# Top-k attention and channel mix on one core: the last 64 rows of two head pairs in two shared tiles

## The chip, the cores and the metric

One core of one Trainium2 chip runs the whole program. The metric is device time in microseconds (us), the median of several runs. TensorE (PE), VectorE (DVE), ScalarE (ACT), GpSimd (POOL) and the DMA queue of SyncE (SP) each work through their own instructions in order; semaphores tie them together.

## What is computed

For 8 batches and 8 heads, with 576 rows of 64 numbers: scores q·kᵀ/8, of each row of 576 scores only those not under the 32nd largest are kept, softmax over them, times v. The heads side by side give x (576 rows of 512), and x goes through a channel mix:

```
scores = scale * q @ k.T;  kth = 32nd largest of each row
attn = softmax(where(scores >= kth, scores, -1e9));  x = attn @ v
xk = mu_k*x + (1-mu_k)*x_prev;  xr = mu_r*x + (1-mu_r)*x_prev
out = sigmoid(xr @ w_r) * (relu(xk @ w_k)**2 @ w_v)
```

x_prev is x one row earlier. Everything is float32; the products of the mix are made of three products of split operands (`three`, lines 630 to 632).

## The kernel before

**Attention in tiles of 128 rows.** Heads go in pairs, so that two times 64 channels fill 128 partitions; a batch has four pairs (`hp`). 576 rows of two heads are nine tiles: tiles 0 to 7 alternate between the heads (head `j = i % 2`, 128 rows each), tile 8 holds the last 64 rows of both heads, one above the other. `visits()` lists the work: for each batch the four pairs with tiles 0 to 3, then the four pairs with tiles 4 to 8 (`HALVES`). That is 64 visits and 288 tiles.

**Scores (L815 to L848).** For tiles i and i+1 one `score` makes two products of 64 contraction rows and 512 columns, one head on the upper 64 rows of the array and one on the lower (L843), into two banks of PSUM (`psA`, `psB`). One `sliver` makes the scores against the last 64 keys of both heads (L839), with keys laid out block-diagonally. For tile 8 `score8` multiplies a block-diagonal q (128 x 128) with all keys, 512 + 64 columns (L830, L831). ACT copies each tile to SBUF (`keep`, L848).

**Selection.** DVE finds the 24 largest through seven pieces (`cand` L853, `best` L855, `drop` L858), ACT and POOL mark what lies below (`count` L867, `below` L869), DVE takes eight more (L870), picks the threshold (L872), ACT makes the exponentials (L875), DVE masks and sums them (`mask`, L878).

**Weighing.** PE turns each tile's weights (`turn`, L883), ACT copies them (`et`, L885). The last 64 columns of a pair of tiles are turned together (`turnl` L892, `el` L894); tile 8 has a `turnl` and an `el` of its own. `weigh` (L912, L913) makes ten products per pair of tiles, j = 0 on the left 64 columns of the array, j = 1 on the right ones, 128 columns each, and for tile 8 ten products of 64 columns. The row sums are inverted and spread (`inv` L922, `inv2` L923, `spread` L929), turned (`turni`, L933), copied by ACT (`ri`: L938 for four tiles, two instructions L939 for tile 8), and `place` (L946, L948 for tile 8) writes x in SBUF. All these exist once for tiles 0 to 3, once for 4 to 7 and once for tile 8.

**The mix.** The 4608 rows of x go in 18 chunks of 256 through `mixes`: POOL and ACT make the mixed inputs and split them (L1012 to L1026), PE makes `hidden` (w_k), `gate` (w_r) and `value` (w_v), which run in one chain in the order of the chunks, DVE multiplies (L1069), a DMA stores (L1073). A chunk needs all four pairs' x for its rows. The weights are decoded at the start (L1108 to L1122).

**What sets the order.** Every step is an operation of a planner (`Plan`) with a lane, a cost, a latency and a key. The planner plays the program through with these numbers, always takes the startable operation of smallest key, and the kernel issues instructions in that order. Keys are tile numbers plus offsets by name (`OFF`, and `FIRST`, `HEAD`, `TAIL` for parts of the run); all of these are numbers tuned outside the kernel. Buffers are fixed slots: two of `K` (keys), two of `qs` (queries), two of `v`; a slot is loaded anew when its last reader is done.

Of the kernel before, what the change touches and what calls it, by code (L numbers as in the profile page):

```python
# [13 lines left out]
U16 = mybir.dt.uint16  # L14
# [7 lines left out]
TOPK = 32  # L22
# [15 lines left out]
OFF = dict(kt=-121.428, kq=29.029, v=64.905, zero=125.157, score=-21.076, score8=-233.323, keep=-111.033, cand=4.395, best=-14.048, drop=-234.145,  # L38
           under=-104.819, count=-7.004, below=-87.858, eighth=7.346, nine=-95.487, exps=-2.384, mask=-112.099, turn=-43.368, et=10.16,
           turnl=-32.999, el=-45.066, weigh=-13.326, inv=-38.077, inv2=-154.266, turni=-65.888, ri=48.604, place=-110.038, lowest=85.255,  # L40
           ranks=-161.631, mu=81.53, nmu=-66.769, changek=202.813, sharek=59.24, addk=295.566, xhk=27.059, xlk=-59.888, sharer=146.441, addr=89.379,
           xhr=64.885, xlr=-19.387, hidden=57.882, relu=-325.908, sq=75.222, r2=42.675, hl=89.124, gate=342.639, gexp=-237.14, value=80.824,
           gated=-51.641, store=-26.275, w=151.463, wabs=-23.359, wshift=5.075, wsign=-219.789, wexp=45.53, wfine=-25.33, whi=-128.231, wmul=141.404,
           spread=-76.068, sliver=-106.383, low=-94.304, lowt=146.639, lowr=-225.937, lowc=25.086, wrest=-67.307, wm=184.027, wput=35.385)
CANDS, BESTS = 0.129, -8.186
STEP, WAT, WSTEP, GATE, VALUE, PACE = 21.948, 3.155, 8.557, 3.863, 3.573, -2.0
HALVES = range(4), range(4, 9)
# [19 lines left out]
BONUS = {("S", "W"): -33.152, ("T", "W"): 18.092, ("R", "W"): -33.936, ("T", "S"): 28.628, ("R", "S"): 41.738, ("W", "S"): -27.081, ("S", "R"): 66.373, ("T", "R"): 53.755, ("W", "R"): 68.359, ("R", "R"): 36.687, ("S", "S"): 46.812, ("R", "T"): 21.687, ("W", "W"): -9.529, ("Z", "S"): -113.211, ("W", "Z"): 44.387, ("S", "T"): -26.18, ("Z", "W"): -40.234, ("Z", "R"): 49.709, ("T", "Z"): 90.229, ("S", "Z"): 15.286, ("R", "Z"): 31.114, ("Z", "Z"): -23.831, ("Z", "T"): -8.059, ("W", "T"): 32.559, ("T", "T"): -8.034}  # L67
# [3 lines left out]
NEAR = dict(PE=142.316, ACT=94.901, DVE=1.447, POOL=234.747, SP=6.125)  # L71
LAST, PEAT = "last", 112
LWAT, LWSTEP = 26.429, -3.165
VWAT, VWSTEP = 1.354, 3.543
AT = [-6.03, -8.616, 62.223, 51.725, 69.632, 81.783, 97.48, 87.342, 134.245, 89.408, 140.491, 139.103, 174.089, 182.425, 241.323, 261.83, 194.143, 348.355]
START = 24
FIRST = dict(kt=5.431, kq=3.152, v=-49.962, zero=-7.051, score=-72.928, score8=-89.904, keep=-50.114, cand=30.564, best=-19.859, drop=129.007,
             under=-50.906, count=-109.448, below=29.13, eighth=12.534, nine=10.971, exps=12.953, mask=59.199, turn=-221.857, et=-50.959,
             turnl=-64.196, el=18.176, weigh=-236.035, inv=-23.695, inv2=12.596, turni=-211.084, ri=84.374, place=-108.496, ranks=22.855, mu=-68.04,
             nmu=-170.249, changek=-72.361, sharek=21.572, addk=-131.096, xhk=-23.566, xlk=38.625, sharer=-60.941, addr=151.697, xhr=148.99,  # L80
             xlr=101.845, hidden=50.53, relu=-47.517, sq=23.585, r2=124.261, hl=36.104, gate=-117.566, gexp=-151.448, value=-38.023, gated=138.744,
             store=164.456, w=-17.631, wabs=-242.464, wshift=-71.332, wsign=-114.016, wexp=-28.894, wfine=-150.111, whi=39.513, wmul=-64.181,
             spread=-19.73, sliver=27.977, wrest=45.495, wm=-182.753, wput=-79.997, low=85.741, lowr=-24.363, lowest=116.236, lowc=87.799,
             lowt=-13.95)
HEAD = dict(sharek=-47.371, zero=154.778, lowt=-23.559, score8=-11.785, store=209.645, el=-79.186, gate=-26.338, turni=91.426, sq=26.461, hl=113.15,
            relu=-47.049, wmul=-27.583, low=-6.219, xhk=61.499, inv=110.857, v=-12.116, gated=-131.363, xlk=16.829, turn=42.663, r2=4.269,
            xlr=16.635, addr=-200.707, ri=-66.902, below=-14.314, best=-24.605, wabs=-59.334, lowr=180.774, sliver=-116.326, nmu=14.466, kq=141.279,
            changek=39.743, count=-13.892, hidden=6.777, addk=-98.359, xhr=95.257, lowc=60.575, eighth=-56.451, w=172.797, kt=1.172, wshift=-10.774,
            wexp=15.565, ranks=119.206, spread=32.638, mask=-44.708, whi=179.551, drop=-62.419, gexp=65.164, keep=-94.404, inv2=-20.263, mu=-116.499,
            weigh=-64.727, turnl=48.3, score=-5.275, under=-90.964, nine=-79.706, place=-5.27, sharer=50.724, et=33.131, wfine=30.879,  # L90
            wsign=-118.488, exps=-49.391, lowest=-68.808, value=60.46, cand=6.626, wrest=5.672, wm=2.948, wput=-29.083)
TAIL = dict(addr=75.077, wshift=-71.426, wexp=88.368, sq=220.928, lowt=-151.351, sliver=-126.01, whi=-14.333, xlk=100.276, xhk=54.542, store=-72.657,
            nine=53.016, best=55.339, lowr=9.427, hl=81.731, turni=-109.29, xhr=45.326, relu=-18.048, kt=30.108, drop=85.184, gate=-36.159,
            score8=-63.376, eighth=-43.894, under=-43.046, inv2=-36.699, v=29.142, w=-96.933, wmul=0.662, wfine=26.729, lowest=-64.048, gexp=123.791,
            score=-32.419, sharek=-17.199, wabs=-168.587, exps=2.264, nmu=-196.418, below=26.843, changek=-82.372, lowc=17.854, inv=270.105,
            low=-26.01, gated=77.754, turnl=33.065, place=59.611, ri=124.319, r2=-54.949, weigh=-98.505, spread=-120.091, kq=-22.273, cand=60.211,
            value=5.334, hidden=-50.412, zero=35.483, ranks=-27.964, mu=85.532, count=39.835, mask=101.415, wsign=37.272, xlr=118.137, keep=-40.713,
            addk=3.005, el=-27.772, sharer=-104.183, turn=-6.619, et=-42.42, wrest=30.561, wm=-111.8, wput=-71.442)
# [4 lines left out]
MORE = dict(xh=2, xl=2, et=5, top=3, el=3, eb=3, sg=3, K=2)  # L103
# [84 lines left out]
class Plan:  # L188
# [236 lines left out]
def topk_attention_channel_mix(ctx: ExitStack, tc: tile.TileContext, q, k, v, mu_kr, w_k, w_v, w_r, out):  # L425
# [355 lines left out]
    def attend(plan, visits, X, pair_sums):  # L781
# [6 lines left out]
        seen = None  # L788

        for p, (b, hp, part) in enumerate(visits):  # L790
# [10 lines left out]
            plan.op(ACT if p == 0 else SP, "kq", at0, 500, 2600, lambda P=P, b=b, hp=hp, lo=lo, hi=hi, issue=issue: issue.dma_start(P.qs.t[:, :hi - lo], q[b, hp, :, lo:hi]), writes=[P.qs])  # L801
            P.v = buf("v")
            plan.op(SP, "v", at0, 500, 3800, lambda P=P, b=b, hp=hp: nc.sync.dma_start(P.v.t, v[b, hp]), writes=[P.v])
# [8 lines left out]
            for i in part:  # L812
                n = at0 + i - P.first
                T = Env()
                T.i, T.P = i, P  # L815
                j, u = i % 2, i // 2 % 2
                if i % 4 == 0 or i == P.first:
                    U = Env()
                    U.i = i
                    U.rs, U.weigh = buf("rs"), []  # L820
                    U.w = 1 if i == 8 else min(part[-1], i | 3) + 1 - i
# [3 lines left out]
                if i == 8:  # L825
                    ps, sl = [buf("psA")], buf("sl")

                    def score8(P=P, ps=ps, sl=sl):
                        qd = P.qs.t[:, MAIN - P.first * 64:WIDE - P.first * 64]
                        return [nc.tensor.matmul(ps[0].t, lhsT=qd, rhs=P.K.t[:, :MAIN], start=True, stop=True),  # L830
                                nc.tensor.matmul(sl.t[:, MAIN:S], lhsT=qd, rhs=P.K.t[:, MAIN:S], start=True, stop=True)]  # L831
# [15 lines left out]
                def keep(T=T, x=ps[j] if i < 8 else ps[0], sl=sl, o=960 if j else 0):  # L847
                    return nc.scalar.activation(T.sc.t, sl.t[:, o:o + S], AF.Copy)  # L848
# [436 lines left out]
```

## Time and profile before

| | |
|---|---|
| median of 3 runs | 1171.61 us (1169.31 to 1172.63) |
| the profiled execution, its own time | 1169.51 us |
| its span, first to last instruction | 1167.7 us |
| PE busy | 1096.4 us (94%) |
| DVE busy | 1068.1 us (91%) |
| ACT busy | 1015.9 us (87%) |
| POOL busy | 934.2 us (80%) |
| DMA engines, mean over the span | 78 GB/s, 91.0 MB |

Busy time is the union of the instructions' recorded intervals, and neighbouring instructions overlap by their fixed latencies, so a share near 100% says that an engine always has something under way, not that it can do no more. An average over the span mixes three stages: a start with the decoding of weights, a long middle with attention and mix together, and an end with the mix alone. So the busy times by stage are read first, then single instructions.

### The profile page before, as it was taken

What the parts mean: (1) busy time and instruction counts of PE and PEld (TensorE: products, weight loads), DVE (VectorE), ACT (ScalarE), POOL (GpSimd) and SP (SyncE); (2) the same over time, 40 slices, a digit from 0 to 9 for tenths busy, and PEclk for the clock granted to TensorE, in tenths of its full rate; (3) what the DMA queues carried; (4) which work ended last, traced back from release to release, by engine and by line L of the source; (5) the groups of instructions that cost most, each with busy time, mean ns of one, the idle gap of its engine ahead of it and who ended that gap; (6) DMA issues with size and microseconds to landing.
All of it is one profiled execution on the core that took longest, in us unless ns stands there. A gap on an engine that the chain in (4) does not pass through costs nothing. (4 is left out here: it accounts for less than half of the span.)

```text
span 1167.7 us, 27723 instructions
## 1 busy us (share of the span) xinstructions
PE 1096.4 (94%) x8593; PEld 860.0 (74%) x8593; DVE 1068.1 (91%) x5773; ACT 1015.9 (87%) x2193; POOL 934.2 (80%) x1185
## 2 busy tenths in 40 slices
PE   3566898999999999999999999999999999999998
PEld 1344676877787777878787878787878787878897
DVE  6999999999999999999999999999999999998600
ACT  5888998989898999989899899999998999898641
POOL 4777997868787888888699888888788869787773
PEclk9877999999999999999999999999999999999999
DMA  8644232222122122221221221221221222120000
GB/s 293 227 146 155 86 99 85 67 65 65 58 75 74 58 62 79 67 72 45 86 78 57 60 71 55 75 76 42 87 76 56 60 72 70 60 75 26 19 19 22
DMA packets 38893, 91.00 MB, mean 78 GB/s; under 512 B 4432, under 2 KB 12624, under 8 KB 38736
## 3 DMA queue, kind: packets, MB, share of 16 engines
q1 hardware_dynamic: 38448, 88.75, 24.0%
q8 instruction: 70, 1.15, 0.4%
q14 instruction: 87, 0.71, 0.2%
q10 hardware_dynamic: 288, 0.39, 0.1%
HBM read 79.69 MB, written 9.44 MB: 76 GB/s over the span
## 5 line engine op out<-in xcount | busy, mean ns | idle before, releaser
L869 POOL TENSOR_TENSOR sg<-sc,sg 128x576 f32<-128x576 f32 x288 | 411.1, 1429 | 87.7 <-ACT sg L867 85.7
L853 DVE MAX8 cand<-sc 128x8 f32<-128x82 f32 (+1 forms) x2016 | 375.2, 230 | 6.3 <-ACT sc L848 5.1
L867 ACT ACTIVATE sg<-sc,seen 128x576 f32<-128x576 f32 x288 | 225.1, 782 | 17.6 <-POOL seen L864 15.8
L875 ACT ACTIVATE se<-sc,seen 128x576 f32<-128x576 f32 x288 | 216.5, 752 | 19.4 <-DVE E L878 18.5
L878 DVE SCALAR_TENSOR_TENSOR E<-sc,seen,se 128x576 f32<-128x576 f32 x288 | 230.7, 801 | 0.3
L848 ACT ACTIVATE sc<-ps 128x576 f32<-128x576 f32 x288 | 185.5, 653 | 41.8 <-DVE E L878 21.7
L883 PE MATMUL rot<-ident,E 128*128 128x128 f32 x1152 | 183.1, 285 | 40.5 <-DVE E L878 21.7
L870 DVE MAX8 top<-sg 128x8 f32<-128x576 f32 x288 | 214.6, 745 | 7.0 <-POOL sg L869 6.7
L883 PEld LDWEIGHTS rot<-ident,E 128*128 128x128 f32 x1152 | 132.9, 144 | 105.4 <-DVE E L878 20.7
L855 DVE MAX8 top<-cand 128x8 f32<-128x56 f32 x864 | 176.1, 205 | 2.4
L885 ACT ACTIVATE et<-rot 128x512 f32<-128x512 f32 x288 | 171.1, 601 | 7.3 <-PE rot L883 6.8
L630 PE MATMUL rot<-xh,wk 128*128 128x256 f32 x576 | 169.6, 294 | 0.0
L912 PE MATMUL ps<-et,v 128*64 128x128 f32 (+1 forms) x2560 | 161.5, 269 | 1.8 <-ACT el L894 1.3
L631 PE MATMUL rot<-xl,wk 128*128 128x256 f32 x576 | 160.9, 279 | 0.3 <-POOL xl L1026 0.3
L632 PE MATMUL rot<-xh,wk 128*128 128x256 f32 x576 | 160.8, 279 | 0.0
L843 PE MATMUL ps<-K,qs 64*128 64x512 f32 x512 | 154.9, 684 | 0.2
L912 PEld LDWEIGHTS ps<-et,v 128*64 128x64 f32 x2560 | 132.8, 139 | 25.0 <-issue 8.5
L630 PE MATMUL rot<-wv,hh 128*128 128x512 f32 x288 | 121.3, 421 | 0.0
L858 DVE MATCH_REPLACE8 cand<-top,cand 128x56 f32<-128x56 f32 x576 | 115.2, 200 | 0.4 <-issue 0.4
L630 PEld LDWEIGHTS rot<-xh,wk 128*128 128x128 f32 x576 | 109.6, 190 | 6.4 <-issue 4.5
L632 PE MATMUL rot<-wv,hl 128*128 128x512 f32 x288 | 113.4, 394 | 0.0
L631 PE MATMUL rot<-wv,hh 128*128 128x512 f32 x288 | 112.6, 391 | 0.0
(87 smaller groups left out, 2303.4 us busy)
## 6 DMA issues: line engine op xcount, KB each, us to landing
v<-in_v SPq DMA_DIRECT2D x64, 384.0 KB, 3.1
K<-in_k SPq DMA_DIRECT2D x64, 352.0 KB, 3.0
out<-eb SPq DMA_DIRECT2D x35, 256.0 KB, 2.0
qs<-in_q SPq DMA_DIRECT2D x32, 192.0 KB, 3.2
stage<-in_moe_w_k SPq DMA_DIRECT2D x8, 512.0 KB, 4.9
xT<-in_moe_w_v SPq DMA_DIRECT2D x8, 512.0 KB, 4.6
stage<-in_moe_w_k SPq DMA_DIRECT2D x8, 511.5 KB, 4.7
xT<-in_moe_w_v SPq DMA_DIRECT2D x8, 511.5 KB, 3.6
```

Of the source, the lines that this page charges most:

```text
L630: return [nc.tensor.matmul(ps, lhsT=sh, rhs=mh, start=first, stop=False), nc.tensor.matmul(ps, lhsT=sh, rhs=ml, start=False, stop=False), ...
L631: nc.tensor.matmul(ps, lhsT=sh, rhs=ml, start=False, stop=False),
L632: nc.tensor.matmul(ps, lhsT=sl, rhs=mh, start=False, stop=last)]
L848: return nc.scalar.activation(T.sc.t, sl.t[:, o:o + S], AF.Copy)
L853: lambda T=T, c=c: nc.vector.max(T.cand.t[:, 8 * c:8 * c + 8], T.sc.t[:, CUTS[c]:CUTS[c + 1]]), reads=[T.sc], writes=[(T.cand, c)])
L867: lambda T=T, sn=sn: nc.scalar.activation(T.side.t, T.sc.t, AF.Sign, bias=sn(T, 1), scale=-BELOW, accum_out=T.top.t[:, TOPK:TOPK + 1]),
L869: plan.op(POOL, "below", n, 1375, 1430, lambda T=T: nc.gpsimd.tensor_mul(T.side.t, T.sc.t, T.side.t), reads=[T.sc], writes=[T.side])
L870: plan.op(DVE, "eighth", n, 660, 754, lambda T=T: nc.vector.max(T.top.t[:, 24:32], T.side.t), reads=[T.side], writes=[(T.top, 3)])
L875: plan.op(ACT, "exps", n, 667, 754, lambda T=T, pe=pe, sn=sn: nc.scalar.activation(pe.t, T.sc.t, AF.Exp, bias=sn(T, 0), scale=SCALE), read ...
L878: lambda T=T, U=U, pe=pe, sn=sn: nc.vector.scalar_tensor_tensor(T.e(), T.sc.t, sn(T, 2), pe.t, op0=OP.is_ge, op1=OP.mult, accum_out=U.rs.t ...
L883: return [nc.tensor.transpose(pt.t[:, c * 128:(c + 1) * 128], E.t[:, o + c * 128:o + (c + 1) * 128], ident) for c in range(NKC)]
L912: return [*[nc.tensor.matmul(pa[hs[j]], lhsT=vs[j][:, c, :], rhs=ms[c][j], start=(c == 0), stop=False) for c in range(NKC) for j in range(2)],
```

## The change

The last 64 rows of two neighbouring pairs (`hp` even and odd) are put in two ordinary tiles, 8 and 9, which are worked on in the visit of the odd pair: tile 8 holds head 0 of both pairs, tile 9 head 1. The count of tiles stays 288. `score8` falls away; the score of tiles 8 and 9 is four products of 64 x 64 on the four quarters of the array, their sliver two products on its column halves. `turnl`, `el`, `inv`, `inv2`, `spread`, `turni`, `ri` and `place` exist once where there were two; the two weighings stand in one operation. `v` and `qs` have three slots, and smaller ones, `K` still two. Twelve transposes of the identity run on PE at the start (`warm`). Costs of DMAs in the planner are raised, and all offsets have new values, among them that of `value`, the last product of the mix, 137.781 for 80.824.

```diff
-HALVES = range(4), range(4, 9)
+HALVES = range(4), range(4, 8)
...
-                vs.append((b, hp, part))
+                vs.append((b, hp, range(part[0], 10) if part[0] and hp % 2 else part))
...
-MORE = dict(xh=2, xl=2, et=5, top=3, el=3, eb=3, sg=3, K=2)
+MORE = dict(xh=2, xl=2, et=5, top=3, el=3, eb=3, sg=3)
...
-            lo, hi = P.first * 64, WIDE if full else (part[-1] + 1) * 64
+            lo, hi = P.first * 64, S if full else (part[-1] + 1) * 64
...
-            plan.op(SP, "v", at0, 500, 3800, lambda P=P, b=b, hp=hp: nc.sync.dma_start(P.v.t, v[b, hp]), writes=[P.v])
+            plan.op(SP, "v", at0, 1150, 3400, lambda P=P, b=b, hp=hp: nc.sync.dma_start(P.v.t, v[b, hp, :, :WIDE]), writes=[P.v])
...
-                if i == 8:
-                    ps, sl = [buf("psA")], buf("sl")
...
-                    plan.op(PE_, "score8", n, 1090, 1280, score8, reads=[P.K, P.qs], writes=[*ps, sl], mode="Z")
-                elif j == 0:
+                ends = [before, P] if i >= 8 else [P]
+                if j == 0:
                     ps, sl = [buf("psA"), buf("psB")], buf("sl")
...
+                        if i == 8:
+                            return [nc.tensor.matmul(to[r * 64:(r + 1) * 64], lhsT=X.qs.t[:, MAIN // 2:MAIN // 2 + REST], rhs=X.K.t[:, S:].rearrange("p (h x) -> p h x", h=2), start=True, stop=True)
+                                    for r, X in enumerate(ends)]
...
+                        if i == 8:
+                            return [nc.tensor.matmul(ps[h].t[ws[r]], lhsT=X.qs.t[w, MAIN // 2:MAIN // 2 + REST], rhs=X.K.t[w, :MAIN], start=True, stop=True)
+                                    for r, X in enumerate(ends) for h, w in enumerate(ws)]
...
-                    plan.op(PE_, "score", n, 965, 1155, score, reads=[P.K, P.qs], writes=ps, mode="S")
+                    plan.op(PE_, "score", n, 965, 1155, score, reads=[x for X in ends for x in (X.K, X.qs)], writes=ps, mode="S")
...
+                    if i < 8:
+                        U.weigh.append((weigh, 1140, [t.et for t in es] + [el, P.v], [U.pa[u]]))
+                    else:
+                        U.weigh.append((lambda weigh=weigh, ends=ends: [x for r, X in enumerate(ends) for x in weigh(P=X, r=r)], 1258, [t.et for t in es] + [el] + [X.v for X in ends], U.pa))
...
+                        if U.i == 8:
+                            return nc.vector.tensor_mul(x.t[:, hp - 1:hp + 1, 1 + MAIN:], pair_sums[:, :, :REST], U.ri.t[:, :128].rearrange("p (u q) -> p u q", u=2))
...
-        sizes = dict(v=(2, [128, WIDE + 2 * D]), K=(2, [128, S + 2 * REST]), qs=(2, [128, 384]), ...
+        sizes = dict(v=(3, [128, WIDE]), K=(2, [128, S + 2 * REST]), qs=(3, [128, MAIN // 2 + REST]), ...
...
+            plan.op("PE", "warm", -99, 1300, 1500, lambda: [nc.tensor.transpose(warm.t[:, :128], ident, ident) for _ in range(12)], writes=[warm], mode="T")
```

## Rows read from the trace of the kernel before

**Rows 1.** Busy us (x instructions): window, its length, PE, PEld, DVE, ACT, POOL; PEclk, DMA, GB/s.

```profile
0.00:200.00 200.00, 137.25 (x909) 93.34 (x910) 184.24 (x894) 166.34 (x347) 152.61 (x183) 0.88 0.48 158
...
200.00:1107.00 907.00, 903.66 (x7346) 717.39 (x7347) 880.56 (x4875) 830.45 (x1814) 748.06 (x975) 1.00 0.21 64
...
1080.00:1107.00 27.00, 27.00 (x224) 22.14 (x224) 17.36 (x77) 17.86 (x41) 19.13 (x24) 1.00 0.03 11
1107.00:1163.00 56.00, 55.47 (x346) 49.30 (x342) 2.98 (x6) 19.06 (x35) 33.50 (x29) 1.00 0.06 20
```

**Rows 2.** Timeline where attention ends: start us, length us, engine, line, what, count.

```profile
1100.24 0.42 DVE L946 TENSOR_TENSOR xT<-ps,ri 128x256 f32<-128x256 f32 x1 [1.95 <-PE ps L913]
...
1105.45 2.55 POOL L1026 TENSOR_TENSOR xl<-xm,xh 128x512 fp32r<-128x512 f32 x2
...
1106.99 0.29 PE L913 MATMUL ps<-el,v 128*64 128x64 f32 x4
1107.21 0.39 PE L630 MATMUL rot<-xh,wk 128*128 128x256 f32 x1
```

**Rows 3.** DVE's `cand`: timeline near the start, and its group by line.

```profile
8.36 1.41 DVE L853 MAX8 cand<-sc 128x8 f32<-128x82 f32 x9 [2.25 <-ACT sc L848]
...
L853 DVE MAX8 cand<-sc 128x8 f32<-128x82 f32 x1440 | 291.7, 229 | 6.3 <-ACT sc L848 5.1
```

**Rows 4.** PE timeline of one `score8` and the transpose that follows.

```profile
535.93 1.02 PE L830 MATMUL ps<-K,qs 128*128 128x512 f32 x2
...
536.96 0.39 PE L933 MATMUL rot<-ident,ri 128*128 128x128 f32 x2
```

**Rows 5.** PE timeline of `turn`, `score`, `sliver` and what follows.

```profile
563.06 0.60 PE L883 MATMUL rot<-ident,E 128*128 128x128 f32 x4
563.59 1.13 PE L843 MATMUL ps<-K,qs 64*128 64x512 f32 x4
564.65 0.49 PE L839 MATMUL ps<-K,qs 128*128 128x128 f32 x2
564.89 0.48 PE L630 MATMUL rot<-wv,hh 128*128 128x512 f32 x1
```

**Rows 6.** PE timeline of single transposes and `weigh` of tile 8; one `weigh` of 128 columns.

```profile
560.53 0.27 PE L933 MATMUL rot<-ident,ri 128*128 128x128 f32 x1
560.64 0.27 PE L892 MATMUL ps<-ident,E 128*128 128x128 f32 x1
560.84 0.69 PE L912 MATMUL ps<-et,v 128*64 128x64 f32 x16
561.36 0.29 PE L913 MATMUL ps<-el,v 128*64 128x64 f32 x4
561.57 0.50 PE L630 MATMUL rot<-wv,hh 128*128 128x512 f32 x1
...
568.63 1.09 PE L912 MATMUL ps<-et,v 128*64 128x128 f32 x16
...
569.77 1.04 PE L912 MATMUL ps<-et,v 128*64 128x128 f32 x16
```

**Rows 7.** Groups by line, engine and shape: busy us, mean ns of one, idle before.

```profile
L948 DVE TENSOR_TENSOR xT<-ps,ri 128x64 f32<-128x64 f32 x32 | 6.9, 217 | 2.3 <-ACT ri L939 1.2 <-ACT sc L848 0.5 <-PE ps L913 0.2
```

**Rows 8.** Loads of K: PE and SP timelines, time to landing, a wait on SP's queue.

```profile
499.68 0.59 PE L830 MATMUL ps<-K,qs 128*128 128x512 f32 x1
...
500.47 0.33 SPq L797 DMA_DIRECT2D K<-in_k  x1
...
DMA to landing us min/median/max: 2.8/3.0/5.7
...
SPq L1073 <- DVE eb L1069: 108.3, 10, 28.7
```

**Rows 9.** PE timeline of the first products.

```profile
4.85 0.77 PE L839 MATMUL ps<-K,qs 128*128 128x128 f32 x2 [4.85 <-DMA qs<-in_q]
5.55 2.08 PE L843 MATMUL ps<-K,qs 64*128 64x512 f32 x4
```

More of the change, by code (lines that the diff above doesn't have):

```diff
@@ L37 @@
 BIG = 3.0e38
[L38 to L46, printed above, removed]
-HALVES = range(4), range(4, 9)
+OFF = dict(kt=-121.077, kq=24.149, v=20.84, zero=149.844, score=-39.01, keep=-107.344, cand=5.903, best=-12.044, drop=-198.58, under=-101.486,
+           count=-24.438, below=-113.606, eighth=8.556, nine=-64.432, exps=-9.366, mask=-113.332, turn=-39.888, et=8.524, turnl=-26.569, el=-78.147,
+           weigh=-20.184, inv=-21.087, inv2=-158.168, turni=-57.394, ri=38.991, place=-111.092, lowest=86.536, ranks=-191.035, mu=107.174,
+           nmu=-58.973, changek=180.472, sharek=80.73, addk=365.911, xhk=20.588, xlk=-31.558, sharer=180.623, addr=83.068, xhr=72.144, xlr=-16.622,
+           hidden=53.798, relu=-284.467, sq=60.178, r2=44.856, hl=62.629, gate=352.164, gexp=-199.494, value=137.781, gated=-34.817, store=-18.263,
+           w=113.339, wabs=-40.251, wshift=-20.817, wsign=-217.528, wexp=65.271, wfine=-66.428, whi=-120.894, wmul=142.464, spread=-58.58,
+           sliver=-128.099, low=-52.865, lowt=184.813, lowr=-246.656, lowc=39.666, wrest=-74.626, wm=213.815, wput=40.232, warm=53.746)
+CANDS, BESTS = 0.017, -2.025
+STEP, WAT, WSTEP, GATE, VALUE, PACE = 20.36, 0.224, 9.64, 3.507, 2.147, -2.0
+HALVES = range(4), range(4, 8)
 EDGE = {}
@@ L70 @@
 WINDOW, PHASE, WARM, COLD = 3413.0, 2079.0, 0.87, 0.58
-NEAR = dict(PE=142.316, ACT=94.901, DVE=1.447, POOL=234.747, SP=6.125)
+NEAR = dict(PE=157.266, ACT=76.938, DVE=1, POOL=261.35, SP=6.558)
 LAST, PEAT = "last", 112
-LWAT, LWSTEP = 26.429, -3.165
-VWAT, VWSTEP = 1.354, 3.543
-AT = [-6.03, -8.616, 62.223, 51.725, 69.632, 81.783, 97.48, 87.342, 134.245, 89.408, 140.491, 139.103, 174.089, 182.425, 241.323, 261.83, 194.143, 348.355]
+LWAT, LWSTEP = 31.888, -6.03
+VWAT, VWSTEP = -1.139, 5.086
+AT = [-5.1, -5.555, 51.008, 47.915, 93.618, 89.398, 100.157, 104.652, 128.392, 109.529, 144.755, 158.616, 187.701, 201.674, 248.803, 270.327, 149.86, 317.867]
@@ L76 @@
 START = 24
[L77 to L98, printed above, removed]
+FIRST = dict(kt=-1.785, kq=-24.691, v=-0.15, zero=65.223, score=-127.556, keep=-16.697, cand=86.654, best=-13.56, drop=90.909, under=-12.036,
+             count=-124.231, below=30.915, eighth=21.203, nine=-26.168, exps=-23.451, mask=-25.825, turn=-292.12, et=-76.879, turnl=-51.926,
+             el=17.542, weigh=-251.388, inv=-46.765, inv2=-4.297, turni=-202.827, ri=96.159, place=-93.665, ranks=-16.354, mu=-84.833, nmu=-180.369,
+             changek=-30.993, sharek=-7.504, addk=-148.701, xhk=-27.565, xlk=-19.55, sharer=-26.546, addr=151.08, xhr=175.741, xlr=145.386,
+             hidden=91.67, relu=-40.596, sq=-27.892, r2=159.509, hl=1.664, gate=-120.618, gexp=-89.376, value=9.741, gated=92.13, store=211.43,
+             w=62.857, wabs=-224.928, wshift=-66.754, wsign=-90.338, wexp=-51.337, wfine=-149.487, whi=68.72, wmul=-39.712, spread=-5.043,
+             sliver=44.517, wrest=41.572, wm=-270.975, wput=-21.368, low=109.06, lowr=-20.378, lowest=-13.413, lowc=116.59, lowt=-44.392, warm=4.784)
@@ new lines @@
+HEAD = dict(sharek=-81.359, zero=157.402, lowt=-40.507, store=231.059, el=-96.218, gate=-33.097, turni=86.301, sq=34.797, hl=95.225, relu=1.438,
+            wmul=-42.825, low=-5.397, xhk=29.602, inv=120.375, v=-41.994, gated=-119.048, xlk=0.56, turn=24.641, r2=9.809, xlr=1.771, addr=-173.981,
+            ri=-84.852, below=-28.723, best=-30.304, wabs=-68.452, lowr=145.302, sliver=-89.717, nmu=-3.799, kq=134.689, changek=26.107,
+            count=-10.486, hidden=42.562, addk=-129.918, xhr=117.728, lowc=69.784, eighth=-51.607, w=175.093, kt=6.492, wshift=-20.148, wexp=28.327,
+            ranks=120.794, spread=40.406, mask=-37.861, whi=185.572, drop=-73.272, gexp=77.992, keep=-132.507, inv2=-19.203, mu=-99.229,
+            weigh=-78.004, turnl=30.848, score=-25.787, under=-82.725, nine=-86.445, place=2.566, sharer=44.352, et=13.205, wfine=33.128,
+            wsign=-100.538, exps=-45.834, lowest=-77.835, value=126.112, cand=-1.741, wrest=11.967, wm=12.618, wput=-20.259, warm=44.126)
@@ new lines @@
+TAIL = dict(addr=85.228, wshift=-91.515, wexp=60.528, sq=202.291, lowt=-139.423, sliver=-154.996, whi=-31.377, xlk=115.629, xhk=87.364,
+            store=-67.526, nine=16.291, best=88.675, lowr=65.433, hl=108.472, turni=-91.253, xhr=65.184, relu=-20.772, kt=26.656, drop=74.773,
+            gate=-75.134, eighth=-47.698, under=-17.213, inv2=-50.015, v=26.911, w=-128.135, wmul=-16.96, wfine=71.971, lowest=-107.655,
+            gexp=124.983, score=-17.478, sharek=-20.476, wabs=-139.355, exps=19.436, nmu=-204.743, below=28.596, changek=-82.112, lowc=-7.223,
+            inv=347.114, low=-41.573, gated=70.169, turnl=21.547, place=60.494, ri=115.522, r2=-59.543, weigh=-121.388, spread=-140.324, kq=-12.827,
+            cand=77.263, value=36.674, hidden=-73.864, zero=78.389, ranks=-37.726, mu=121.68, count=62.15, mask=106.892, wsign=17.424, xlr=105.738,
+            keep=-25.734, addk=23.028, el=-41.818, sharer=-126.165, turn=6.939, et=-42.814, wrest=48.199, wm=-163.754, wput=-79.388, warm=-10.03)
@@ L772, in prep_all @@
         P.v = g.two.tile([128, WIDE + 2 * D], F32, name="v_in")
-        for to, x in ((P.K, k), (P.q, q), (P.v, v)):
+        for to, x in ((P.K, k), (P.v, v), (P.q[:, :MAIN], q[..., :MAIN])):
             nc.sync.dma_start(to, batch(x)[hp])
+        nc.gpsimd.memset(P.q[:, MAIN:], 0.0)
+        for h in range(2):
+            w = slice(h * 64, (h + 1) * 64)
+            nc.sync.dma_start(P.q[w, MAIN + h * REST:MAIN + (h + 1) * REST], batch(q[..., w, MAIN:])[hp])
     def new_batch(g):
@@ L787, in attend @@
         xT = {}
-        seen = None
+        seen = before = None
         for p, (b, hp, part) in enumerate(visits):
@@ L848, in keep @@
+                    plan.op(PE_, "sliver", n, 230, 420, sliver, reads=[x for X in ends for x in (X.K, X.qs)], writes=[sl], mode="T")
+                def keep(T=T, x=ps[j], sl=sl, o=960 if j else 0):
                     return nc.scalar.activation(T.sc.t, sl.t[:, o:o + S], AF.Copy)
-                plan.op(ACT, "keep", n, 530, 648, keep, reads=[ps[j] if i < 8 else ps[0], sl], writes=[T.sc])
+                plan.op(ACT, "keep", n, 530, 648, keep, reads=[ps[j], sl], writes=[T.sc])
                 for c in range(NCH):
@@ L914, in attend @@
-                    cost = 1140 if i < 8 else 629
-                    U.weigh.append((weigh, cost, [t.et for t in es] + [el], U.pa[u]))
+                        vr = P.v.t[:, MAIN:WIDE].rearrange("p (j d) -> p j d", j=2)
+                        o, m = (0, 128) if r is None else (r * 64, 64)
+                        pa = U.pa[u if r is None else r].t[:, :m]
+                        return [*[nc.tensor.matmul(pa[hs[j]], lhsT=vs[j][:, c, :], rhs=es[j].et.t[:, c * 128 + o:c * 128 + o + m], start=(c == 0), stop=False) for c in range(NKC) for j in range(2)],
+                                *[nc.tensor.matmul(pa[hs[j]], lhsT=vr[:, j], rhs=el.t[:, o:o + m], start=False, stop=True) for j in range(2)]]
@@ L1073, in store @@
                     issue.dma_start(rows[t:t + m], G.e.t[:m])
-                plan.op(ACT if end else SP, "store", k1, 600, 2500, store, reads=[G.e])
+                plan.op(ACT if end else SP, "store", k1, 900, 2500, store, reads=[G.e])
     def weights(plan, X):
```

108 lines of the change are left out of this document (43 added, 65 removed).

## Prediction

> **What bounds the kernel now.** I read the busy times by stage first [rows 1]. From 200 us to 1107 us PE is busy 903.66 of 907 us at the full clock, DVE 880.56 (97%), ACT 830.45, POOL 748.06. So in the long middle PE is under way without a break, DVE nearly so. From 1107 us to 1163 us PE is again full (55.47 of 56) and the rest hardly works: these are the last two chunks of the mix. Only the first 200 us leave PE idle (200 − 137.25 = 62.75 us), at a mean granted clock of 0.88; there DVE is the fullest (184.24). Next I ask whether DVE is a second wall. Nine `cand` follow each other in 1.41 us, 0.157 each, while a single one is recorded with 0.229 [rows 3]: each recorded interval covers 0.07 us in which the next is already running, so DVE's 97% overstates its load. PE's figure has the same flaw, but on PE I can check the streams: in [rows 5, 6] every product begins where the one before has streamed, except for short pauses at changes of array form, which are priced below. Last I look at the seam between attention and the end: `place` for tiles 4 to 7 of the last pair comes at 1100.24, the split inputs of the next chunk are made from 1105.45 on, the last `weigh` ends on PE, and the chunk's first product starts at 1107.21 [rows 2]. The seam is tight on both sides: PE had work until then, and the inputs came just then. In the last 27 us of attention DVE has 17.36 us of work [rows 1], so there PE's queue, not DVE, sets the pace. My reading: PE's total work sets the time from 200 us on, and attention must finish earlier too if a gain on PE is to reach the end.
>
> **The change part by part, for two pairs of one batch; there are 16 such places.** All prices are start to start at the full clock.
>
> *Scores.* Removed: two `score8`. One takes from 535.93 to 536.96 [rows 4], 1.03 us; two 2.06. Added: the quarter score. Not in the trace; its nearest row is the score on two halves: 563.59 to 564.65, 1.06 us, plus the pause ahead of it. Four transposes started at 563.06 and take 0.11 each (560.53 to 560.64) [rows 6], so they have streamed at 563.50, and the pause is 0.09. If all four quarters stream at once, 1.15 us. If only two do, another 1.06: 2.21. I take 1.15, because both kinds of side by side are in the trace. Two row halves: four records of 512 columns in 1.06 us [rows 5], where `score8` needs 1.03 for half as many of the same length (and two short ones). Two column halves: a `weigh` of twenty records of 128 columns takes 568.63 to 569.77, 1.14 us, 0.057 a record [rows 6], while a full-array transpose of 128 columns takes 0.11. Added: a sliver, 0.24 us on the full array (564.65 to 564.89) [rows 5]; as two streams on column halves the same if they run together, 0.48 if not, and 0.10 for the change of form behind it, taken from the 0.09 pause; 0.34 to 0.58, I take 0.34. Together 2.06 − 1.15 − 0.34 = 0.57 us saved; by the bad ends 2.06 − 2.21 − 0.58 = −0.73.
>
> The Trainium skill (TensorE: Matmul & The Clock Gate, Part 3: Packing small matmuls) speaks against this part: by it a weight load overlaps running products only when its row group differs, and here two quarters share each row group. By that rule the second column half would wait, and the sum here would be −0.49 instead of +0.57. The `weigh` row speaks against it, for its two column halves share all rows and still run at 0.057 us a record; no run here shows four quarters.
>
> *Weighing.* The twenty records of 64 columns stay twice, but in one operation. One alone: `turnl` starts 560.64, has streamed at 560.75, and the mix goes on at 561.57 [rows 6]: 0.82 us. Sixteen of its records take 0.52, so twenty more in the same form add 0.65. Saved 0.82 − 0.65 = 0.17; between 0 and 0.25.
>
> *Turns.* One `turnl` and one `turni` less, 0.11 each [rows 6]: 0.22.
>
> *PE in all:* 0.57 + 0.17 + 0.22 = 0.96 us a place, 15.4 us for 16; bounds +1.04 (16.6 us) and −0.51 (−8 us).
>
> *Other engines.* One `el`, `inv`, `spread`, `inv2` less and three ACT copies; `place` once instead of twice: DVE loses at least one L948, 0.217 us [rows 7], some 0.3 with the reciprocal, 4 to 5 us in 16 places. ACT and POOL lose more, but both have 77 us and more of idle time in the middle [rows 1], so I count nothing. DMA: `v` and the longer `qs` shrink by a sixth (640 for 768 columns, 320 for 384); the DMA engines are busy 21% of the middle [rows 1]: nothing.
>
> *The seam.* Tiles 8 and 9 now both follow `place` of tiles 4 to 7 in the last visit. One tile takes on average 1107/288 = 3.8 us, so the chunk that waits for that `place` [rows 2] is released with one tile more of attention still to come: up to 3.8 us in favour, and the last chunk has the 28 us of the one before it as cover for the later `place`. This is what lets attention's side of the seam follow; I add nothing for it.
>
> *Start.* `warm` puts twelve transposes ahead of PE's first products, which wait 4.85 us for the queries [rows 9]. The first score takes 2.08 us against 1.13 later [rows 9, 5], so PE runs at the lower level there. At twice 0.11 the twelve take 2.6 us: hidden by that wait, and 2.6 us if it were gone. Should it raise the clock for two scores, 2 us; I take nothing.
>
> *Order anew, `value` later, raised costs of DMAs, third slots of `v` and `qs`.* No row prices these. What a better or worse order has to win or lose is the idle time of DVE: 15.8 us in the first 200, 26.4 from there to 1107, 9.6 of them in the last 27. I allow 8 us either way around zero; `value` yielding to attention should help the seam and costs nothing while other PE work is queued.
>
> **The sum.** Two of the 16 places fall in the first 200 us, where PE has idle time, so their 1.9 us do not count: 15.4 − 1.9 = 13.5 us. For this attention must go 1.5% faster, DVE from 97.1% to 98.5% of the recorded kind, which by [rows 3] is room that exists. The profiled execution took 1169.5 us: 1156.0. It lies 2.1 us below the median of the runs, so for a median I forecast 1158 us. Its own range, with 16.6 us and 3.8 of the seam at one end and half the gain lost to DVE at the other, is 1151 to 1165.
>
> **Rivals.**
> 1. *Attention does not go faster.* DVE is the wall after all; PE gets idle spots in the middle and only DVE's 4 to 5 us less work and part of the seam count. For: 97% recorded, seam tight. Against: the overlap in [rows 3]. 1171.6 − 6 = 1166.
> 2. *The quarters go two by two.* The score costs 2.21; a place saves 2.06 − 2.21 − 0.34 + 0.17 + 0.22 = −0.10, 14 places cost 1.4 us: 1173. That is also the case in which the change doesn't do what it says. It is the case of the rule named above, and I give it little for the `weigh` row.
> 3. *Slower: K comes late.* K keeps two slots, and now both are held until the quarter score. Before, K was issued 0.8 us after `score8` (499.68, 500.47) [rows 8] for the visit after the next, a whole visit ahead. After the change the very next visit needs it: 1.15 us of score, some 0.4 to issue, 3.0 to land [rows 8], 4.5 us in all, while the next score is due on average two tiles, 7.7 us, later. The cover is 3 us. SP's queue is in order: a store that waits for DVE ahead of it (10 waits, 108.3 us [rows 8]) would hold K up, and PE's queue stands behind a late K with all products of the mix. It decides from 13.5/15 = 0.9 us of PE wait at each of the 15 places; at 2 us each, 30 − 13.5 = 16.5 us slower: 1188.
> 4. *A worse order elsewhere* eats the gain, or a better one adds: within 8 us of the forecast either way, 1150 to 1166, nearly inside the first range; beyond it, about 1171.
>
> **Chances.** Forecast 0.64 (1151 to 1165), rival 1 0.15, rival 2 0.07, rival 3 0.08, rival 4 beyond the range 0.06. About 0.3% (3.5 us, so 1168.1 to 1175.1) is what a measurement of this kernel can tell from no change. Faster: 0.64 + 0.13 of rival 1 + 0.02 = 0.79; same: 0.02 + 0.06 + 0.03 = 0.11; slower: 0.10. Predicted 1158; range 1147 to 1170: it takes in 4 us of a better order below and rival 1 above, and leaves out rivals 2 and 3 and the bad tail.
>
> **What would show it.** PE's records: the eight records of 512 columns of a quarter score in 1.1 us (two by two: 2.1), no pause of more than 0.1 us around its sliver. PE still full from 200 us to the end, with about 15 us less busy time; DVE's share of the middle up by a point. The seam some 12 us earlier. Wrong: PE idle in the middle with DVE unchanged (rival 1), waits of the sliver or score for a DMA of K (rival 3), or a start that takes longer.

## The result, and the profile after

The changed kernel takes 1152.89 us (median of 4 runs, 1152.23 to 1154.79) against 1171.61 us for the kernel before (median of 3); the ratio is 0.9846 with an interval from 0.9824 to 0.9869. A few executions are far slower whatever the kernel (one of the kernel before took 3696.18 us); these are left out, here and in every run below. The forecast was 1158 us with a range from 1147 to 1170, so the sign and the range held, and the gain came out about a third larger (18 us by the ratio for 13.5).

One statement ahead of the prediction is wrong and has to be corrected first. The section on the change says that `K` keeps two slots, and the line of its diff that begins with `sizes` shows `K=(2, ...`. In the kernel after that line reads `K=(3, [128, S + 2 * REST])`: the keys have three slots. Rival 3 of the prediction was built on the wrong line; what two slots would really do was then tried (two_K_slots below).

The changed kernel by stage, with the columns of [rows 1]:

```profile
0.00:200.00 200.00, 146.16 (x972) 101.00 (x973) 188.26 (x906) 169.55 (x348) 156.69 (x186) 0.86 0.47 159
200.00:1107.00 907.00, 903.85 (x7459) 713.02 (x7458) 872.02 (x4832) 825.19 (x1766) 753.84 (x954) 1.00 0.18 58
```

The last but one chunk of the mix waits for the `place` at 1100.24 us before [rows 2] and at 1080.46 after. The kernel before, from its start to that `place`:

```profile
0.00:1100.24 1100.24, 1034.15 (x8208) 805.32 (x8209) 1063.55 (x5765) 992.52 (x2148) 895.50 (x1151) 0.98 0.26 81
```

The kernel after, likewise:

```profile
0.00:1080.50 1080.50, 1023.51 (x8227) 790.35 (x8228) 1055.51 (x5721) 980.38 (x2083) 887.71 (x1118) 0.97 0.24 78
```

Two accounts of the same 19.7 us can be read from the last two. By DVE: 1063.55 to 1055.51 is 8.0 us less work in front of the seam (fewer `place` and reciprocals, and one tile more that now lies behind it), and its idle time falls from 36.7 to 25.0, another 11.7. By PE: 1034.15 to 1023.51 is 10.6 less, and idle time falls from 66.1 to 57.0, 9.1 less, most of it in the first 200 us (62.75 in [rows 1], now 200 − 146.16 = 53.84).

The seam, to be read beside [rows 2]: timelines of DVE, POOL and PE.

```profile
1080.46 0.43 DVE L943 TENSOR_TENSOR xT<-ps,ri 128x256 f32<-128x256 f32 x1 [0.22 <-PE ps L908]
...
1085.55 1.30 POOL L1023 TENSOR_TENSOR xl<-xm,xh 128x512 fp32r<-128x512 f32 x1
...
1088.20 0.29 PE L908 MATMUL ps<-el,v 128*64 128x64 f32 x4
1088.42 0.39 PE L629 MATMUL rot<-xh,wk 128*128 128x256 f32 x1
```

The chunk's first product starts at 1088.42 for 1107.21, 18.8 us earlier. The seam is as tight as before: inputs from 1085.55 on, the last `weigh` done just ahead.

PE around one quarter score (L836 is its sliver, L843 the score, L894 a `turnl`) and around one `weigh` of tiles 8 and 9:

```profile
504.25 0.39 PE L631 MATMUL rot<-wv,hl 128*128 128x512 f32 x1
504.56 0.44 PE L836 MATMUL ps<-K,qs 128*64 128x128 f32 x4
504.93 0.66 PE L885 MATMUL rot<-ident,E 128*128 128x128 f32 x4
505.43 0.27 PE L894 MATMUL ps<-ident,E 128*128 128x128 f32 x1
505.63 1.09 PE L843 MATMUL ps<-K,qs 64*64 64x512 f32 x8
506.65 0.39 PE L629 MATMUL rot<-xh,wk 128*128 128x256 f32 x1
...
529.72 0.27 PE L930 MATMUL rot<-ident,ri 128*128 128x128 f32 x1
529.93 0.69 PE L907 MATMUL ps<-et,v 128*64 128x64 f32 x16
530.44 0.29 PE L908 MATMUL ps<-el,v 128*64 128x64 f32 x4
530.56 0.64 PE L907 MATMUL ps<-et,v 128*64 128x64 f32 x16
531.02 0.29 PE L908 MATMUL ps<-el,v 128*64 128x64 f32 x4
531.24 0.39 PE L629 MATMUL rot<-xh,wk 128*128 128x256 f32 x1
```

Eight records of 512 columns take 505.63 to 506.65, 1.02 us: all four quarters stream at once, as fast as two halves did (1.06, [rows 5]). The two weighings take 529.93 to 531.24, 1.31 us.

### The profile page after: what moved, and what is told of

Read it like the earlier page. It is cut to its first block, busy times and chain, and to the rows that moved or that the text cites. A ratio compares the mean times of both kernels' runs of the same rounds, so it can differ in the third digit from the quotient of the medians.

```text
span 1151.1 us, 27634 instructions
## 1 busy us (share of the span) xinstructions
PE 1087.1 (94%) x8637; PEld 846.3 (74%) x8637; DVE 1063.0 (92%) x5741; ACT 1004.4 (87%) x2129; POOL 927.2 (81%) x1153
## 3 DMA queue, kind: packets, MB, share of 16 engines
q8 instruction: 70, 1.15, 0.4%
## 5 line engine op out<-in xcount | busy, mean ns | idle before, releaser
L855 DVE MAX8 cand<-sc 128x8 f32<-128x82 f32 (+1 forms) x2016 | 379.8, 231 | 5.5 <-ACT sc L850 4.0
L629 PEld LDWEIGHTS rot<-xh,wk 128*128 128x128 f32 x576 | 108.9, 189 | 12.9 <-issue 8.5
```

The costliest lines, as they stand in the source:

```text
L629: return [nc.tensor.matmul(ps, lhsT=sh, rhs=mh, start=first, stop=False), nc.tensor.matmul(ps, lhsT=sh, rhs=ml, start=False, stop=False), ...
L855: lambda T=T, c=c: nc.vector.max(T.cand.t[:, 8 * c:8 * c + 8], T.sc.t[:, CUTS[c]:CUTS[c + 1]]), reads=[T.sc], writes=[(T.cand, c)])
```

## The experiments

The theory at the start was A: PE's work, plus the time that PE lies idle in the first 200 us, sets the end. Against it stood B, the new order makes the gain and the shared tiles do not, and C, DVE is the wall. Times of experiments are medians, ratios are to the kernel before in the same session. The kernel before took 1170.7 to 1172.3 us in these sessions, so differences to the changed kernel (1152.89) are good to some 2 us.

**1. Old tiles with the new numbers**

All tuned numbers (`OFF`, `CANDS`, `STEP`, `BONUS`, `NEAR`, `AT`, `FIRST`, `HEAD`, `TAIL` and others) and the planner's costs of DMAs are those of the kernel after; two of the lines:

```diff
-CANDS, BESTS = 0.129, -8.186
+CANDS, BESTS = 0.017, -2.025
...
-NEAR = dict(PE=142.316, ACT=94.901, DVE=1.447, POOL=234.747, SP=6.125)
+NEAR = dict(PE=157.266, ACT=76.938, DVE=1, POOL=261.35, SP=6.558)
...
```

> The kernel before with its tile 8 and score8, but all tuned numbers and DMA costs of the kernel after (score8 keeps its own offsets), and no warm. Theory A (PE's work plus PE's idle time at the start set the end): the products of score8 stay (35.4 us of PE against 23.5 in the changed kernel), the start may be better by up to 7.5 us as in the changed kernel: 1164 to 1170. Theory B (the new order makes the gain, the shared tiles do not): 1153 to 1158. Numbers made for other tiles may also lose: above 1175 would say that they only fit their own tiles.

1189.84 us, ratio 1.0158 (1.0138 to 1.0178): 19 us slower than before. This is the third case of the expectation: the numbers only fit their own tiles.

**2. New tiles with the old numbers behind tile 48**

```diff
-        o.key = grid(o.base + OFF[name] + ...
+        o.key = grid(o.base + (OFF if o.base < 48 or name not in OFF2 else OFF2)[name] + ...
```

`OFF2` has the offsets of the kernel before; `BONUS`, `NEAR`, `AT` and `TAIL` are that kernel's too, while `STEP`, `GATE`, `VALUE` and the costs of DMAs stay new. This mixture was tuned for neither kernel.

> The kernel after, but with the tuned numbers of the kernel before for all steps behind tile 48, with that kernel's numbers for the mix and the switches of form; the first 48 tiles, the weights and warm keep the new numbers. Theory A: PE has its smaller work, some 10 us of the gain of 18 stay, 1158 to 1163. Theory B: 1165 to 1172.

1178.97 us, ratio 1.0072 (1.0054 to 1.0090): 8 us slower than before and 26 us slower than the changed kernel, though it has the smaller work on PE. A and B foresaw neither of the two. Against the same tiles with their own numbers run 1 loses 19 us and run 2 loses 26 us: an edit that makes the planner find another order measures the order at least as much as the edit. So 1 and 2 can't split the gain, and from here on the order of the changed kernel was held and instructions were added to it or taken from it.

**3. No transposes at the start**

```diff
-lambda: [nc.tensor.transpose(warm.t[:, :128], ident, ident) for _ in range(12)]
+lambda: []
```

> The kernel after in the same order, without the twelve transposes at the start. If they are hidden by the wait for the queries and change no clock: 1152 to 1154, no difference. If they are what makes the first 45 tiles end 7.5 us earlier: 1158 to 1161.

1153.05 us, ratio 0.9850 (0.9833 to 0.9868): no difference. PE's first products, first of the kernel after, then without the transposes:

```profile
1.42 2.82 PE L1165 MATMUL rot<-ident 128*128 128x128 f32 x12 [1.42 <-POOL ident masks.py:199]
4.64 0.77 PE L838 MATMUL ps<-K,qs 128*128 128x128 f32 x2 [0.40 <-DMA qs<-in_q]
5.33 2.08 PE L845 MATMUL ps<-K,qs 64*128 64x512 f32 x4
```

```profile
4.49 0.77 PE L838 MATMUL ps<-K,qs 128*128 128x128 f32 x2 [4.49 <-DMA qs<-in_q]
5.18 2.08 PE L845 MATMUL ps<-K,qs 64*128 64x512 f32 x4
```

The twelve are hidden by the wait for the queries, and the first score takes 2.08 us with or without them, so no higher clock shows there.

**4. Two slots for the keys**

```diff
-K=(3, [128, S + 2 * REST])
+K=(2, [128, S + 2 * REST])
```

> The kernel after with two slots for the keys instead of three, planned with the same numbers. The next visit's keys are then issued only when the quarter score is done; they take some 4.5 us from its start, and in the changed kernel the next score starts 6.9 us or more after it. If that cover holds: 1153 to 1156. If the loads come late behind waiting stores and PE's queue stands, by 2 us at each of 15 places: 1175 to 1190.

1166.76 us, ratio 0.9969 (0.9955 to 0.9983): 14 us of the gain go, which is in neither case of the expectation. But not by late keys. Who waited for the loads of K, and their landing, in this run:

```profile
who waited for it (us, times):
  PEld ps L838: 0.8, 1
...
DMA to landing us min/median/max: 2.8/3.3/5.2
```

One wait of 0.8 us in the whole run, as many as with three slots. The planner knew of the missing slot and made another order, with numbers found for three slots; that the loss lies in that order, as in 1 and 2, is my reading and not shown by itself. What a third slot is worth with numbers of its own was not tried.

**5. The quarter score twice, in the same order**

```diff
-for r, X in enumerate(ends) for h, w in enumerate(ws)]
+for _ in range(2) for r, X in enumerate(ends) for h, w in enumerate(ws)]
```

> The kernel after in its own order, with each quarter score issued twice, the second over the first: 16 times 1.02 us of PE more, 16.3 us, which is about what two score8 cost more than one quarter score. If PE's work sets the time: 13 to 17 us more, 1166 to 1170. If DVE or the order sets it and PE has room: 1153 to 1157. These extra products also stand before the scores of tiles 8 and 9, so a part may come from their delay.

1164.57 us, ratio 0.9942 (0.9921 to 0.9964): 11.7 us more than the kernel after (the 12.3 us in the next expectation should read so), between the two cases of the expectation. The next run's rows, which double this score too, show its price: 511.54 to 513.42 is 1.88 us for 1.02, so 16 places added 13.8 us and not 16.3. 11.7/13.8 = 0.85 us of time for each us of PE (0.82 by the ratios, 0.9942 − 0.9846 of 1172).

**6. The end steps twice, in the same order**

This is meant to put the spared work back. Quarter score, `turnl`, `el`, `spread`, `turni`, `ri` and `place` of tiles 8 and 9 are each issued twice.

```diff
-return nc.scalar.activation(U.ri.t[:, :m * 128], pr.t[:, :m * 128], AF.Copy)
+return [nc.scalar.activation(U.ri.t[:, :m * 128], pr.t[:, :m * 128], AF.Copy) for _ in range(1 + (U.i == 8))]
...
```

> The kernel after in its own order, with the work that the shared tiles spare put back for tiles 8 and 9: quarter score, turnl, el, spread, turni, ri and place each issued twice (per place some 1.2 us of PE, 0.3 of ACT, 0.3 of POOL, 0.2 to 0.3 of DVE). The quarter score twice alone cost 12.3 us. If the spared work is what the gain is made of: 1168 to 1173, that is, all of the 18 us go back. If only the scores' place in front of tiles 8 and 9 mattered: 1164 to 1167, as with the score alone.

1170.61 us, ratio 1.0005 (0.9995 to 1.0016). PE around a doubled score in this run:

```profile
511.34 0.27 PE L894 MATMUL ps<-ident,E 128*128 128x128 f32 x1
511.54 1.95 PE L843 MATMUL ps<-K,qs 64*64 64x512 f32 x16
513.42 0.39 PE L629 MATMUL rot<-xh,wk 128*128 128x256 f32 x1
```

With the doubled steps the new order takes as long as the old kernel. That agrees with A in the sum, but it does not show that the gain was made of spared work. First, it is not a copy of the old work: PE's busy time rises by 13.4 us (1087.1 to 1100.6) where the change had lowered it by 9.3, `inv` and `inv2` can't be issued twice, and the sliver and the joined `weigh` stayed as they are. Second, run 8 will show that products which have nothing to do with the tiles cost nearly as much for each us of PE, so B is not out. Third, the time goes back elsewhere than it was won. Each kernel masks 288 tiles, 36 to a batch, so the 72nd `mask` in order of time marks two batches of tiles done, and the 252nd seven, in all three. Both, in the kernel before, the kernel after and this run:

```profile
312.21 0.81 DVE L878 SCALAR_TENSOR_TENSOR E<-sc,seen,se 128x576 f32<-128x576 f32 x1
960.44 0.80 DVE L878 SCALAR_TENSOR_TENSOR E<-sc,seen,se 128x576 f32<-128x576 f32 x1
```

```profile
304.15 0.81 DVE L880 SCALAR_TENSOR_TENSOR E<-sc,seen,se 128x576 f32<-128x576 f32 x1
946.32 0.80 DVE L880 SCALAR_TENSOR_TENSOR E<-sc,seen,se 128x576 f32<-128x576 f32 x1
```

```profile
307.03 0.81 DVE L880 SCALAR_TENSOR_TENSOR E<-sc,seen,se 128x576 f32<-128x576 f32 x1
962.15 0.81 DVE L880 SCALAR_TENSOR_TENSOR E<-sc,seen,se 128x576 f32<-128x576 f32 x1
```

The spans end at 1167.7, 1151.1 and 1168.9 us. By stretch of the profiled executions:

| stretch | places with tiles 8 and 9 | change wins | run 6 loses again |
|---|---|---|---|
| start to the 72nd `mask` | 4 | 8.1 us | 2.9 us |
| 72nd to the 252nd | 10 | 6.1 us | 13.0 us |
| 252nd to the end of the span | 2 | 2.5 us | 2.0 us |

Half of the gain is there after two of the eight batches, and the doubled steps take little of that back; in the next five batches they cost twice what the change had won. That the sums meet is in part luck. Run 6 prices added work in this order, and does not show where the gain comes from.

**7. and 8. Less and more work on PE, outside attention**

In the gates of chunks 0 to 7 the third of three products is left out, or a fourth is added: 64 products of 0.23 us, 14.6 us.

```diff
-for y in three(pz.t[:m], ...
+for y in (two if c < 8 else three)(pz.t[:m], ...   # run 8: four for two
```

> The kernel after in its own order; the gates of chunks 0 to 7 leave out the third of their three products (64 products of 512 columns, 0.23 us each, 14.6 us of PE, all before 610 us and none of them in attention). If PE's work sets the time and attention can follow: 8 to 15 us less, 1138 to 1145. If DVE is the wall: at most 4 us less, 1149 to 1153.

> The kernel after in its own order; the gates of chunks 0 to 7 make a fourth product (low part by low part), 14.6 us of PE more, none of it in attention. Taking away as much had given 0.6 us. If PE is a wall in this order only against more work: 10 to 15 us more, 1163 to 1168. If PE has room outside the scores and the quarter score twice was dear for its place ahead of tiles 8 and 9: 1153 to 1157.

With two products it takes 1152.31 us (ratio 0.9835, 0.9818 to 0.9851), 0.6 us less. With four it takes 1165.79 us (0.9955, 0.9939 to 0.9972), 12.9 us more, 0.88 for each us of PE, about the price of the score. Busy times in the stretch with these chunks (columns of [rows 1]), of the kernel after, then with two products, then with four:

```profile
160.00:610.00 450.00, 447.38 (x3678) 349.68 (x3678) 447.05 (x2491) 418.92 (x900) 376.42 (x480) 1.00 0.20 67
```

```profile
160.00:610.00 450.00, 439.11 (x3636) 337.34 (x3635) 447.68 (x2498) 419.95 (x901) 377.69 (x481) 1.00 0.20 66
```

```profile
160.00:610.00 450.00, 447.73 (x3665) 351.80 (x3665) 437.06 (x2428) 408.74 (x873) 364.82 (x467) 1.00 0.21 66
```

With less to do PE falls idle (439.11 of 450) and DVE does no more than before (447.68); with more to do PE stays full and DVE, ACT and POOL starve (437.06). PE bounds this order against more work, and something else holds it when PE has less.

**9. The same in the kernel before**

> The kernel before in its own order; the gates of chunks 0 to 7 leave out the third of their three products, 14.6 us of PE. The prediction's reading (PE's total work sets the time of the kernel before): 8 to 15 us less, 1157 to 1163. The reading after the runs on the changed kernel (attention, paced by DVE, sets the time, and PE is filled to fit): 0 to 2 us less, 1169 to 1172.

1170.41 us, ratio 0.9996 (0.9984 to 1.0008): nothing. Busy times of the kernel before, then of this run:

```profile
160.00:610.00 450.00, 442.64 (x3592) 345.81 (x3591) 444.48 (x2467) 417.00 (x908) 372.97 (x486) 1.00 0.23 70
160.00:610.00 450.00, 436.30 (x3547) 337.02 (x3545) 445.62 (x2474) 418.08 (x912) 374.55 (x487) 1.00 0.23 71
```

PE idles 13.7 of 450 us there, 7.4 in the kernel before, and the time is the same. The prediction's reading that PE's total work sets the time does not hold for less work in a given order. What an order planned anew for the smaller work would make of it was not tried.

**10. More work on DVE**

```diff
-lambda T=T, sn=sn: nc.vector.scalar_tensor_tensor(T.nine.t, ...),
+lambda T=T, sn=sn, i=i: [nc.vector.scalar_tensor_tensor(T.nine.t, ...) for _ in range(2 if i % 2 == 0 else 1)],
```

> The kernel after in its own order; the step that picks the threshold on DVE is issued twice for every even tile, 144 times 0.14 us, 20 us of DVE more. If DVE is the wall: about 20 us more, 1170 to 1174. If PE is the wall and DVE has the room that its overlapping records suggest (4% of the middle): 3 to 10 us more, 1156 to 1163.

1183.51 us, ratio 1.0091 (1.0070 to 1.0112): 30.6 us more, beyond both cases of the expectation. The price was set too low: each extra step brings the reading of its accumulator with it (DVE's instructions go from 5741 to 6029, 288 more), and DVE's busy time grew from 1063.0 to 1091.4, 28.4 us. So about 1.1 us of time go with each us of DVE: more work on DVE costs in full as well. (The step also stands in the chain of the selection; whether its delay there adds to the price was not tested.)

**11. and 12. Less work on DVE, and on both**

In batches 1 to 7 the masking of tiles 0, 4 and 8 leaves out half of its columns, 70 times 0.3 us; in run 12 the gates of chunks 0 to 7 also have two products.

```diff
-T.e(), T.sc.t, sn(T, 2), pe.t, op0=OP.is_ge ...
+T.e()[:, :w], T.sc.t[:, :w], sn(T, 2), pe.t[:, :w], op0=OP.is_ge ...   # w = S // 2 if b and i % 4 == 0 else S
```

> The kernel after in its own order; in batches 1 to 7 the masking step of tiles 0, 4 and 8 does 288 of its 576 columns, 70 times 0.3 us, 21 us of DVE less. If DVE alone paces attention: 15 to 21 us less, 1132 to 1138. If PE stands as a second wall right behind it: 3 to 8 us less, 1145 to 1150.

> The kernel after in its own order with both: half masks in 70 tiles (21 us of DVE less) and two products in the gates of chunks 0 to 7 (14.6 us of PE less). If DVE alone paces: as with the half masks alone, 1131 to 1138. If PE is a second wall right behind: clearly below the run with half masks alone, by 6 to 14 us.

1149.80 us (ratio 0.9826, 0.9810 to 0.9843) and 1147.72 us (0.9800, 0.9782 to 0.9817): 3.1 us less for 21 us of DVE, 5.2 us less for those and 14.6 us of PE. Run 11 falls in the case of two walls, run 12 in neither of its cases. The middle in the kernel after and in run 12:

```profile
200.00:1080.00 880.00, 876.85 (x7254) 689.02 (x7254) 866.97 (x4815) 810.83 (x1736) 730.52 (x933) 1.00 0.18 59
```

```profile
200.00:1080.00 880.00, 870.85 (x7216) 680.31 (x7215) 855.95 (x4825) 810.43 (x1739) 732.12 (x935) 1.00 0.19 60
```

With both engines relieved neither is full (PE idles 9.2 us, DVE 24.1), and the stretch holds hardly more of DVE's instructions (4825 for 4815). So neither PE nor DVE alone, nor the two together, pace this order: C falls as A did. What does was not found. My reading, not shown: instructions stand in fixed queues and wait for each other across engines, the planner has filled PE and DVE to nearly the same height, and relief in one place ends at the next wait. The longest waits of run 12 in total are POOL's for ACT's `count` (85.4 us), and POOL has idle time to spare. ACT and POOL were relieved in no run, so they stay open as rivals.

## Why the prediction was right, and where it was not

*The quarters.* Right: 1.02 us and a pause of 0.09 (`turnl` at 505.43 has streamed by 505.54), 1.11 us for the 1.15 taken. Rival 2 falls. The rule of the Trainium skill behind it (TensorE: Matmul & The Clock Gate, Part 3: Packing small matmuls) does not hold here. The weight loads of the quarter score at 505.63:

```profile
505.63 0.21 PEld L843 LDWEIGHTS ps<-K,qs 64*64 64x64 f32 x8 [0.17 <-issue]
```

All eight lie within 0.21 us, while the first products run (they begin at 505.63 and the last of the eight products ends 1.09 us later), so quarters that share a row group loaded and ran together.

*The removed `score8`.* Undersized. I read 1.03 us from one place; from each record's start to the next over all 32 they took 35.4 us, 1.11 each. The sliver was undersized too: 504.56 to 504.93 and a pause ahead of it (the product at 504.25 streams 0.23), 0.45 for 0.34. Summed so over all places, scores and slivers of the last rows went from 35.4 to 23.5 us: 0.75 a place for the 0.57 taken.

*Weighing and turns.* The weighing in one operation saves 0.82 × 2 − 1.31 − 0.10 = 0.23 us at the place shown, for 0.17. But over the whole kernel all weighings went only from 176.2 to 175.0 us, and `turnl` and `turni` together from 44.7 to 46.1: there are fewer of them, but 102 of the 144 `turnl` now stand just ahead of a `score` or a `weigh`, 83 of 160 before, and bear the pause (505.43 to 505.63, 0.20 for 0.11). I had counted 0.22 a place as saved. The term was lost in the new order.

*PE in all.* Predicted 15.4 us, measured 12.1: busy time fell by 9.3 us (1096.4 to 1087.1), with 2.8 us of new transposes in it.

*The step from PE's work to time.* I said that PE's total work sets the time from 200 us on. In a held order runs 7 and 9 speak against it: 14.6 us less of PE's work, away from attention, gave 0.6 and 0.3 us, within what the medians can tell. Runs 5, 6 and 8 price work that is added at 0.8 to 0.9 us for each us of PE, and do not tell what spared work is worth. No run takes PE's work out of attention alone, and run 11, which takes DVE's work out of steps that attention waits for, gave 3.1 of 21 us. What speaks for my step is the changed kernel itself: behind the 72nd `mask` PE is nearly as full as before (7.4 us idle before, 9.9 after), and 8.5 us of time went with some 11 us less of PE's busy time. So the step is neither shown nor refuted for an order that was planned anew, which is the case it was made for.

*The seam and DVE.* The seam moved by 18.8 us, more than the 12 forecast, while DVE's recorded share rose less than I had it: from 200 us to 1080 us 866.97 of 880 (98.5%) for 863.20 (98.1%); the 97.1% of the prediction took in the thin last stretch. The 8.0 us less of DVE work in front of the seam, some 3 of them one tile that now lies behind it, I had not counted for the time.

*Start and order.* I took nothing, with 8 us either way. This is the step that failed, and the number hides it. Up to the 72nd `mask` (2 batches of 8) the change wins 8.1 us, before and after:

```profile
0.00:313.05 313.05, 249.17 (x1814) 181.61 (x1815) 295.53 (x1506) 270.66 (x570) 245.01 (x307) 0.92 0.38 124
```

```profile
0.00:305.05 305.05, 250.97 (x1854) 182.85 (x1855) 292.83 (x1498) 266.42 (x556) 242.78 (x299) 0.91 0.37 125
```

PE is busy 1.8 us longer there, with the 2.8 us of the new transposes, and idles 54.1 us for 63.9. So by PE's account this half of the gain is less idle time and not less work: the good side of rival 4. Behind it the change wins 8.5 us, where 12 places at 0.96 us had been forecast as 11.5. A term at nothing that measured 8 and a term that was too large make up for each other in part; that the median lies only 5 us from the forecast is in part luck. What made the start faster stays open. The 72nd `mask`, at 312.21 before and 304.15 after, starts at 303.67 without `warm` (run 3), so the transposes are not it. It starts at 311.23 with the new numbers on the old tiles (run 1) and at 313.15 with the new tiles and slots but old numbers (run 2), so neither alone brings it; with two slots for the keys (run 4) it starts at 306.38, so most of it does not hang on the third. More can't be told apart, since every edit of slots or numbers changes the whole order.

*Rival 3.* Its premise was misread, as said above. Even with two slots the keys were not late (run 4), so its mechanism is refuted. That run was slower than the kernel after by 14 us all the same, with another order.

## What to carry to other kernels

A full engine in a profile shows that more work there will cost; it does not show that less work there will pay: here, with the order held, one more us of PE cost 0.8 to 0.9 us and one less gave under 0.1. When a kernel's order comes from a planner with tuned numbers, hold the order when you test a cause, by issuing a step twice or leaving products out; a plan with other numbers or slots alone moved this kernel by 14 to 26 us. But a step issued twice prices added work only. To see where a gain comes from, compare the times at which the kernels have done the same counted amount of work. Price a removed step from all its places, start to start, and look at which steps bear the pauses at a change of array form afterwards.

## What the runs showed of the hardware

Four 64 x 64 quarters stream four products of 512 columns in float32 (eight records) in 1.02 us; the first four records start between 505.62 and 505.65. Two 64 x 128 halves take 1.06 us. Issued twice, the second set follows in 0.86 us without a new pause (511.54 to 513.42). A change of array form costs a pause of 0.08 to 0.10 us at the places shown (563.50 to 563.59 in [rows 5], 504.48 to 504.56, 505.54 to 505.63, 529.83 to 529.93). In the first 10 us of the kernel after the row grants the full clock:

```profile
0.00:10.00 10.00, 6.89 (x22) 4.43 (x24) 2.20 (x16) 2.48 (x3) 0.91 (x10) 1.00 0.81 283
```

Yet the score there takes 2.08 us, 1.13 later. By its duration it ran near the lower of the two levels; the granted clock of this row does not show it.
